# Spectral and gated mixer: the opening in a written order, S1 and S2 ahead of S3 and S4, and four down blocks moved into the last plain call

## The chip, the core and the metric

The kernel runs on one core of a Trainium2 chip. The metric is device time of one execution in microseconds: a median of 3 runs of the kernel, and beside it one profiled execution, whose span runs from its first to its last instruction. Five engines work side by side, each taking its own instructions in order: TensorE (PE in the profile, its weight loads PEld), VectorE (DVE), ScalarE (ACT), GpSimd (POOL) and SyncE (SP), which here only issues transfers.

## The reference

```python
def _A_ref(x, w_r, w_i):              # B, S, D = 1, 2048, 576
    X = rfft2(x, axes=(-2, -1)) * (w_r + 1j * w_i)
    return irfft2(X, s=(S, D), axes=(-2, -1))

def _B_ref(x, w_gate, w_up, w_down):  # F = 4608
    g = einsum("bsd,df->bsf", x, w_gate)
    u = einsum("bsd,df->bsf", x, w_up)
    return einsum("bsf,fd->bsd", sigmoid(g) * u, w_down)

xn = layernorm(x, axis=-1)            # eps = 1e-5
return x + _A_ref(xn, w_r, w_i) + _B_ref(xn, w_gate, w_up, w_down)
```

The spectral part is done as matrix products with Fourier matrices late in the kernel and is not touched by the change.

## The kernel before

Everything is kept to float32 accuracy out of products in a shorter format: each operand is split into a rounded high part and a low part. ScalarE writes the high part (a copy that rounds), VectorE the low part (operand less high part). A contraction over half of D, 288, takes seven matmuls (the list STEPS of `prod`, L648): two blocks of 128 with high by high, low by high and high by low, and one last step, (2, 2), on a **remainder** block, in which the 32 columns that are left stand three times, as high, high and low.

The 2048 rows of x form two pairs of chunks of 512 rows, four tiles of 128 rows each. A tile is read to `acc` (L358); VectorE takes its mean and variance (L369, L370); `scales` (L374 on) makes factor and bias, with a square root on ScalarE; `prep_hi` (L420) normalises on ScalarE into the buffer `xa`; `rem_hi` and `rem_lo` (L402, L407) make the remainder part `rma` or `rm`. `fill` (L449 to L455) then transposes two tiles on TensorE into a pair of PSUM banks (tag "pp", two such pairs, shared with the down blocks and the spectral part): four transposes of the main columns and two of the remainder. ScalarE copies the main block (L453) and the remainder (L454) into the operand store `X`, and VectorE writes the low part (L455), which frees the pair.

The 36 column blocks of F are the units. For units 0 and 1 of each pair of chunks `plain` (L671 to L677) is called once for each chunk: four products, two for the gate (bank A or B) and two for the other factor (bank E), then a sigmoid, a multiplication and the two parts of h (`hh`, `hl`). In the first pair of chunks the calls are (unit 0, chunk 1), (1, 1), (0, 2), (1, 2), here called the first to the last plain call. From unit 2 on `unit` (L699 to L739) works on both chunks at once with seven products in place of eight, on the blocks A11, A12, A22 of X and the sums S1 = A21 + A22, S2 = S1 - A11, S3 = A11 - A21, S4 = A12 - S2. `sums` (L432 to L435) makes these in place in `xa`. S3 takes the place of A21 in X, so it is filled after the plain calls.

Two units' h go through `down` (L755): for one tile of 128 rows 12 matmuls with w_down into a pair of banks, the **down block**; VectorE adds it to `acc` (L759). There are eight for the first two units, one for each tile; before, all start in unit 2. Weights come raw by transfer (L238), are split by `parts` (L250 on ScalarE, L252 and L254 on VectorE) into `w`, and are written to HBM for the second pair. `w_down` goes the same way (L304, L309, L311).

The program is recorded in one order and a scheduler may move instructions of an engine against each other. `placed` and `keep_in_program_order` mark instructions that must keep the recorded order. `beside(i)` and `turn` run the side jobs (weights, fills, sums, additions) between the products of a call. Ahead of the first products TensorE multiplies identity matrices (L904, L922), whose results are not used.

## Time and profile before

| | |
|---|---|
| median of 3 runs | 1418.17 us (1417.57 to 1419.64) |
| the profiled execution: its time | 1417.6 us |
| its span | 1415.8 us |
| granted TensorE clock, mean | 0.999 |
| DVE busy | 1123.7 us, 79% of the span |
| ACT busy | 640.3 us, 45% |
| first instruction of the first identity matmul | 3.46 us |
| fourth plain call's last product, followed by unit 2's first | 50.07 us |
| first down block | 61.37 us |

A line of the order of time gives start, time, engine, source line, operation, what it writes and from what, with shapes; "x4" joins equal neighbours, and the bracket is the engine's idle time before and who ended it. A line of a stage gives its bounds and length, then busy time (and instructions) of PE, PEld, DVE, ACT and POOL, the granted clock, the share of DMA engines and GB/s. A line of a group has the least, median and longest duration in ns.

### The profile page before, as it was taken

How to read it: one execution, taken by the hardware profiler on the slowest of the kernel's cores; microseconds unless marked ns; L12 is line 12 of the kernel's file. 1: busy time of each engine (PE TensorE's matmuls, PEld its weight loads, DVE VectorE, ACT ScalarE, POOL GpSimd, SP SyncE). 2: the span in 40 equal slices, each digit the busy share in tenths (PEclk: the TensorE clock that was granted, in tenths of full speed). 3: DMA queues.
4: the chain of work that ended last, by engine and by line, in shares of the span. 5: the costliest groups of instructions: out<-in, count | busy, mean ns of one | idle time of the engine just before them, and what ended most of it. 6: DMA issues, size and time to landing. Idle time of an engine off the chain costs nothing. (4 is left out here: it accounts for less than half of the span.)

```text
span 1415.8 us, 20731 instructions
## 1 busy us (share of the span) xinstructions
PE 1400.5 (99%) x7883; PEld 1228.9 (87%) x7883; DVE 1123.7 (79%) x1736; ACT 640.3 (45%) x1035; POOL 3.3 (0%) x5
## 2 busy tenths in 40 slices
PE   7999999999999999999999999999999999999998
PEld 5888888888888888888888888888888889888887
DVE  7988888888888888789466888877878878777885
ACT  6644444444444444444245444434555534443431
POOL 0000000000000000000000000000000000000000
PEclk9999999999999999999999999999999999999999
DMA  7588677777777776665777777778888787776643
GB/s 251 194 330 306 257 271 261 271 261 270 262 270 261 272 262 243 246 250 176 274 213 237 225 234 222 219 244 266 274 269 271 241 278 223 242 221 205 194 127 84
DMA packets 131043, 342.54 MB, mean 242 GB/s; under 512 B 12192, under 2 KB 51648, under 8 KB 126208
## 3 DMA queue, kind: packets, MB, share of 16 engines
q1 hardware_dynamic: 130016, 339.91, 71.7%
q8 instruction: 62, 1.02, 0.3%
q10 hardware_dynamic: 928, 1.31, 0.3%
q14 instruction: 37, 0.30, 0.1%
HBM read 205.04 MB, written 136.13 MB: 241 GB/s over the span
## 5 line engine op out<-in xcount | busy, mean ns | idle before, releaser
L648 PE MATMUL pB<-X,w 128*128 128x512 f32 x1484 | 381.0, 394 | 0.9 <-ACT pB L699 0.5
L648 PEld LDWEIGHTS pB<-X,w 128*128 128x128 f32 x1484 | 267.4, 188 | 51.7 <-ACT v L712 1.3
L648 PE MATMUL pE<-X,w 128*128 128x512 f32 x1064 | 272.3, 392 | 0.1
L648 PE MATMUL pA<-X,w 128*128 128x512 f32 x1008 | 259.3, 392 | 1.8 <-DVE X L455 1.2
L648 PEld LDWEIGHTS pE<-X,w 128*128 128x128 f32 x1064 | 193.1, 188 | 35.1 <-DVE y L713 0.7
L648 PEld LDWEIGHTS pA<-X,w 128*128 128x128 f32 x1008 | 182.7, 188 | 35.2 <-DVE X L455 1.9
L755 PE MATMUL po<-wd,hh 128*128 128x288 f32 x1216 | 210.8, 295 | 0.0
L846 PEld LDWEIGHTS ps<-wf,hs 128*128 128x128 f32 x1260 | 188.6, 188 | 18.5 <-ACT qs L854 0.9
L846 PE MATMUL ps<-wf,hs 128*128 128x288 f32 x1260 | 202.0, 295 | 0.4 <-ACT qs L854 0.4
L755 PEld LDWEIGHTS po<-wd,hh 128*128 128x128 f32 x1216 | 184.2, 188 | 11.7 <-ACT hh L738 0.4
L759 DVE TENSOR_TENSOR acc<-acc,po 128x576 f32<-128x576 f32 x168 | 125.7, 749 | 65.4 <-PE po L755 64.9
L250 ACT ACTIVATE w<-raw 128x768 fp32r<-128x768 f32 (+1 forms) x106 | 100.9, 953 | 92.6 <-PE pE L648 36.5
L755 PE MATMUL po<-wd,hl 128*128 128x288 f32 x608 | 128.7, 293 | 0.0
L856 DVE TENSOR_TENSOR qs<-qs,ps 128x576 f32<-128x576 f32 x112 | 84.0, 750 | 25.4 <-PE ps L846 24.4
L755 PEld LDWEIGHTS po<-wd,hl 128*128 128x128 f32 x608 | 98.7, 189 | 0.0
L713 DVE TENSOR_TENSOR y<-v,pE 128x512 f32<-128x512 f32 x68 | 46.6, 686 | 50.3 <-ACT v L712 49.5
L733 DVE TENSOR_TENSOR y<-y,g 128x1024 f32<-128x1024 f32 x67 | 81.9, 1222 | 3.4 <-DVE y L732 0.5
L782 ACT ACTIVATE hs<-y 128x512 fp32r<-128x512 f32 x105 | 64.8, 629 | 43.4 <-DVE y L820 14.8
L252 DVE TENSOR_TENSOR w<-raw,w 128x512 fp32r<-128x512 f32 (+1 forms) x106 | 81.8, 772 | 3.2 <-ACT w L250 2.9
L856 DVE TENSOR_TENSOR acc<-acc,ps 128x576 f32<-128x576 f32 x90 | 67.4, 750 | 19.5 <-PE ps L846 18.6
L716 ACT ACTIVATE g<-pB 128x512 f32<-128x512 f32 x68 | 40.7, 598 | 91.3 <-PE pB L648 91.3
L712 ACT ACTIVATE v<-pB 128x512 f32<-128x512 f32 x68 | 40.6, 597 | 70.5 <-PE pB L648 70.2
(170 smaller groups left out, 1611.0 us busy)
## 6 DMA issues: line engine op xcount, KB each, us to landing
w<-wsp SPq DMA_DIRECT2D x246, 320.0 KB, 3.6
wsp<-w SPq DMA_DIRECT2D x34, 2240.0 KB, 7.8
raw<-in_w SPq DMA_DIRECT2D x34, 768.0 KB, 9.6
wdsp<-wd SPq DMA_DIRECT2D x36, 576.0 KB, 4.6
wf<-tsp SPq DMA_DIRECT2D x60, 288.0 KB, 3.5
wf<-wdsp SPq DMA_DIRECT2D x45, 288.0 KB, 3.9
std<-in_wd SPq DMA_DIRECT2D x36, 288.0 KB, 5.5
ri<-in_ri SPq DMA_DIRECT2D x16, 580.0 KB, 5.1
```

The costliest lines, as they stand in the source:

```text
L250: placed(nc.scalar.activation(o[:, :, :3, :], src, AF.Copy))
L252: placed(nc.vector.tensor_tensor(o[:, :, 3:, :], src[:, :, :KT, :], f32(o[:, :, :KT, :]), op=OP.subtract))
L648: nc.tensor.matmul(bank, w[:, sw, :], X[:, x, sx, :], start=start and j == 0, stop=stop and j == len(STEPS) - 1, skip_group_check=skip)
L712: nc.scalar.activation(v[:, 1], bank["B"], AF.Copy)
L713: nc.vector.tensor_tensor(y[:, 1], v[:, 1], bank["E"], op=OP.add)
L716: nc.scalar.activation(g[:, 1], bank["B"], AF.Sigmoid)
L733: nc.vector.tensor_tensor(y, y, g, op=OP.mult)
L755: nc.tensor.matmul(pd[:, b, :HD], h[i], w[k][b], start=g == 0 and n == 0, stop=g == G - 1 and n == 2)
L759: nc.vector.tensor_tensor(a, a, pd[:, :, :HD], op=OP.add)
L782: nc.scalar.activation(hs[:, 0], src, AF.Copy)
L846: nc.tensor.matmul(pd[:, i, :HD], h[:, a, m], w[:, b], start=q == 0, stop=q == 2)
L856: nc.vector.tensor_tensor(o, o, pd[:, :, :HD], op=OP.add)
```

## The change

It touches the code up to unit 2. Six things are done:

1. **Order of the first transfers.** The first raw weights, half (2, 4), are read after two tiles of x instead of after four; the other half after four.
2. **A written opening.** `opening` replaces the first two plain calls and what stood before them. While `strict` is set, `strictly` keeps products, transposes, copies and most small operations in the written order on their engine. The main columns of A11 and A12 are transposed and copied first (`lift`); the remainders of all four tiles follow later in one bank for each operand (`lift_rem`), in the middle of the first plain call. Two pairs of half groups of identity matmuls become 15 and 10 full ones.
3. **Scales.** The square root takes eps as its bias, so VectorE's addition is no longer ahead of it, and the second chunk has two groups of two tiles instead of one group of four.
4. **`plain_late`**, used for the first and third plain call: each of the four products does six steps, the low part of X last, and the four remainder steps come at the end. The third call's gate has half a pair of banks, so the first two gates come later.
5. **S1 and S2 ahead of S3 and S4.** `sums` is divided into `sums_12` and `sums_34`, and the fills of S3 and S4 follow in four steps. Both w_down blocks are made in the third call.
6. **Down blocks.** `pend` holds the four tiles of the first chunk in the last plain call, one for each of its four products, and only the other four in unit 2.

```diff
+    def strictly(ins):
+        if strict[0]:
+            tc.keep_in_program_order(ins)
...
+    LOW_LAST = ((0, 0), (1, 1), (0, 3), (1, 4), (3, 0), (4, 1))
...
+    def plain_late(u, c, beside, mid):
+
+        G_, bank = new_plain(u, c)
+        beside(-1)
+        for i, (b, k) in enumerate(((0, 1), (0, 2), (1, 1), (1, 2))):
+            prod(bank[b], *of_plain(u, c, b, k), k == 1, False, steps=LOW_LAST)
+            end()
+            mid(i)
+            if i < 3:
+                beside(i)
+        for b in range(2):
+            for k in (1, 2):
+                prod(bank[b], *of_plain(u, c, b, k), False, k == 2, steps=STEPS[-1:])
+            if b == 0 and (u, c) != (0, 0):
+                gate(G_, bank)
+        beside(3)
+        return G_, bank
...
-            nc.scalar.activation(w0, ve, AF.Sqrt)
-            nc.vector.reciprocal(r0, w0)
+            strictly(nc.scalar.activation(w1, mv[:, ts, 1], AF.Sqrt, bias=nmr[:, NT - 1:]))
+            strictly(nc.vector.tensor_scalar(ve, mv[:, ts, 1], EPS, -0.5, op0=OP.add, op1=OP.mult))
+            strictly(nc.vector.reciprocal(r0, w1))
...
-    for i in range(TPP):
-        new_acc(0, i)
-        if i in (TPC - 1, TPC + 1):
-            load_raw(i // TPC)
+    for todo in ((new_acc, 0, 0), (new_acc, 0, 1), (load_raw, 0, 2), (new_acc, 0, 2), (new_acc, 0, 3), (load_raw, 0, 0),
+                 (new_acc, 0, 4), (new_acc, 0, 5), (load_raw, 1, 2), (load_raw, 1, 0), (new_acc, 0, 6), (new_acc, 0, 7)):
+        todo[0](*todo[1:])
...
+        identity(15)
+        scaled(0, 0)
+        early(0, 2)
+        level(0, 0)
+        scaled(0, 1)
+        p1 = pair("px_A11")
+        p2 = [ps.tile([P, CW], F32, tag="bE", name=f"px_A12_{i}", bufs=2) for i in range(2)]
+        his, lows = both(0, 0, (p1[:, 0], p2[0]))
+        for f in his:
+            f()
+        identity(10)
+        level(0, 1)
+        next(W[0, 2])
...
+        for m in range(TPC):
+            rem_hi(m, 0, "rm34", TPC)
+        next(W[0, 0])
+        for m in range(TPC):
+            rem_lo(m, 0)
...
+        first = plain_late(0, 0, lambda i: None, mid)
+        load_raw(2)
+        keep_p(0)
...
+            if p == 0 and n == 3:
+                pend = [(0, 0, m) for m in range(TPC)]
...
-                for _ in range((0, 0, 2, 2, 0)[i] if p and n < 2 else 0):
+                for _ in range(int(i >= 0) if p == 0 else (0, 0, 2, 2, 0)[i] if n < 2 else 0):
...
-        pend = [(p, 0, m) for m in range(TPP)]
+        pend = [(p, 0, m) for m in range(0 if p else TPC, TPP)]
```

Three places show how instructions move. In the rows `xa` is a tile's normalised buffer, `px` a bank that transposes write, `rs` the small tile of the scales, `pA`, `pB`, `pE` and `pg` the banks of products, `po` a down block; "x12" counts equal neighbours.

ScalarE from the first square root, before:

```order
L378 ACTIVATE rs_230<-rs_230 128x2
L420 ACTIVATE xa_0_218<-acc,nmr,rstd 128x576
L420 ACTIVATE xa_1_219<-acc,nmr,rstd 128x576
L402 ACTIVATE rma_0_0_240<-xa_0_218 128x2x64
L402 ACTIVATE rma_1_0_243<-xa_1_219 128x2x64
L378 ACTIVATE rs_255<-rs_255 128x2
L453 ACTIVATE X<-px_A_0_264 128x2x256
L454 ACTIVATE X<-px_A_0_264 96x256
L453 ACTIVATE X<-px_A_0_274 128x2x256
L454 ACTIVATE X<-px_A_0_274 96x256
L420 ACTIVATE xa_2_220<-acc,nmr,rstd 128x576
```

and now:

```order
L372 ACTIVATE rs_225<-mv,nmr 128x2
L257 ACTIVATE w_200<-raw_182 128x2x384
L414 ACTIVATE xa_196<-acc,nmr,rstd 128x576
L414 ACTIVATE xa_197<-acc,nmr,rstd 128x576
L372 ACTIVATE rs_244<-mv,nmr 128x2
L437 ACTIVATE X<-px_A_252 128x2x256
L437 ACTIVATE X<-px_A_0_253 128x2x256
L414 ACTIVATE xa_198<-acc,nmr,rstd 128x576
L414 ACTIVATE xa_199<-acc,nmr,rstd 128x576
L437 ACTIVATE X<-px_A_252 128x2x256
```

The remainder parts (`rma`) and remainder copies (96x256) have left this stretch, and a weight conversion stands ahead of the first normalisation.

TensorE from the second group of identity matmuls to the end of the first plain call, before:

```order
L922 MATMUL b_195<-idr 128x512 x4
L449 MATMUL px_A_1_300<-idf,xa_2_220 128x128 x2
L449 MATMUL px_A_1_310<-idf,xa_2_220 128x128 x2
L450 MATMUL px_A_1_300<-idr,rma_2_0_289 96x128
L449 MATMUL px_A_1_300<-idf,xa_3_221 128x128 x2
L450 MATMUL px_A_1_300<-idr,rma_3_0_293 96x128
L450 MATMUL px_A_1_310<-idr,rma_2_0_289 96x128
L449 MATMUL px_A_1_310<-idf,xa_3_221 128x128 x2
L450 MATMUL px_A_1_310<-idr,rma_3_0_293 96x128
L648 MATMUL pA_0_351<-X,w_296 128x512 x14
L648 MATMUL pE_0_352<-X,w_296 128x512 x14
L648 MATMUL pB_0_452<-X,w_360 128x512 x14
```

and now, where `px_r` holds remainders:

```order
L934 MATMUL b_195<-idr 128x512 x10
L434 MATMUL px_A_252<-idf,xa_198 128x128 x2
L434 MATMUL px_A_252<-idf,xa_199 128x128 x2
L434 MATMUL px_A_1_254<-idf,xa_198 128x128 x2
L434 MATMUL px_A_1_254<-idf,xa_199 128x128 x2
L648 MATMUL pA_0_309<-X,w_200 128x512 x12
L648 MATMUL pE_0_310<-X,w_200 128x512 x6
L443 MATMUL px_r_331<-idr,rm_0_294 96x128
L443 MATMUL px_r_331<-idr,rm_0_296 96x128
```

and, behind the other transposes of this kind,

```order
L443 MATMUL px_r_331<-idr,rm_0_300 96x128
L648 MATMUL pE_0_310<-X,w_200 128x512 x6
L648 MATMUL pA_0_309<-X,w_200 128x512 x2
L648 MATMUL pE_0_310<-X,w_200 128x512 x2
L648 MATMUL pB_0_356<-X,w_201 128x512 x14
```

The remainder transposes of all four tiles now stand behind 18 product matmuls of the first call, and the 14 matmuls of a bank are 12 or 6 and 6, with the two remainder steps at the end.

TensorE in the last plain call (`pB_1`, `pE_1`) from the third of the moved down blocks, now (before, the last call held the S1 and S2 transposes and no down block):

```order
L648 MATMUL pE_1_568<-X,w_201 128x512 x4
L788 MATMUL po_2_642<-wd_526,hh_454 128x288 x4
L788 MATMUL po_2_642<-wd_526,hl_455 128x288 x2
L788 MATMUL po_2_642<-wd_528,hh_473 128x288 x4
L788 MATMUL po_2_642<-wd_528,hl_474 128x288 x2
L434 MATMUL px_S_1_660<-idf,xa_198 128x128 x2
L434 MATMUL px_S_1_660<-idf,xa_199 128x128 x2
L443 MATMUL px_S_1_660<-idr,rma_3_598 96x128
L443 MATMUL px_S_1_660<-idr,rma_3_631 96x128
L648 MATMUL pE_1_568<-X,w_201 128x512 x7
L648 MATMUL pA_705<-X,w_590 128x512 x3
```

and VectorE at the same place, up to the part that the S1 transposes wait for:

```order
L438 TENSOR_TENSOR X<-px_S_0_555,X 128x2x256
L792 TENSOR_TENSOR acc<-acc,po_0_577 128x576
L259 TENSOR_TENSOR w_590<-raw_352,w_590 128x3x256
L261 TENSOR_TENSOR w_590<-raw_352,w_590 32x3x128
L402 TENSOR_TENSOR rma_3_598<-xa_198,rma_3_598 128x2x32
L281 TENSOR_TENSOR raw_352<-raw_352 128x2x384
L792 TENSOR_TENSOR acc<-acc,po_1_610 128x576
L283 TENSOR_TENSOR raw_352<-raw_352 128x384
L261 TENSOR_TENSOR w_590<-raw_352,w_590 32x2x128
L284 TENSOR_TENSOR raw_352<-raw_352 128x384
L259 TENSOR_TENSOR w_590<-raw_352,w_590 128x2x256
L402 TENSOR_TENSOR rma_3_631<-xa_199,rma_3_631 128x2x32
```

The S1 transposes of tiles 2 and 3 (`xa_198`, `xa_199`) need the remainder part `rma_3_631`, which on VectorE now has two additions of down blocks (`acc`) and most of unit 2's weights (`w_590`) ahead of it; before, no addition stood there.

More of the change, by code (lines that the diff above doesn't have):

```diff
@@ L282, in make_w, with keep_p @@
         yield
[L284 to L291 removed]
+    def keep_p(f):
+        nc.sync.dma_start(wsp[f][:, :4 * 5 * P], f32(WS[f][:, :4]).rearrange("p a k m -> p (a k m)"))
     def get_w(u):
@@ new lines, in lift_rem, with fill @@
+    def lift_rem(k, ms, rest, srcs=None):
+        for j, m in enumerate(ms):
+            src = srcs[j] if srcs else XR[m, XP[k]]
+            strictly(nc.tensor.transpose(rest[:KR, j * P:(j + 1) * P].bitcast(F32R), src, idr))
+        o = X[:KR, XA[k], KT, ms[0] * P:(ms[-1] + 1) * P]
+        return lambda: strictly(nc.scalar.activation(o, rest[:KR, :len(ms) * P], AF.Copy))
+    def fill(k, mm):
+        pt = pair(f"px_{k}_{mm}")
+        hi, lo = lift(k, mm, pt[:, 0])
+        rest = lift_rem(k, (2 * mm, 2 * mm + 1), pt[:, 1])
+        hi()
+        rest()
+        lo()
@@ L923, in spectral_glu_kernel, with identity @@
-    for m in (2, 3):
-        prep(0, m, 0)
-    next(mk)
-    next(mk)
-    for k in ("A11", "A12"):
-        fill(0, k, 1)
-    for _ in mk:
-        pass
-    stats([acc[TPC + m] for m in range(TPC)], TPC, R["pool"], table=True)
+    idle = [True]
+    def identity(n):
+        for _ in range(n):
+            strictly(nc.tensor.matmul(b0, idr, eye, start=idle[0], stop=True, skip_group_check=True))
+            idle[0] = False
+    for m in range(TPC):
+        new_xs(m)
+    W = {}
+    for f in range(G):
+        w = new_w(f)
+        for i in (2, 0):
+            W[f, i] = parts(w, RAW[f][:, i:i + 2], i, 2)
@@ L1102, in turn @@
     def turn(n):
+        was, strict[0] = strict[0], False
         for _ in range(n):
@@ L1109, in turn @@
         sides[:] = [g for g in sides if next(g, sides) is not sides]
+        strict[0] = was
     def finish(*gs):
```

295 lines of the change are left out of this document (160 added, 135 removed).

## Prediction

> **What bounds the kernel now.** I read the busy times first, then busy time by stage, then the order of time on TensorE, and last the order of time of the engines that TensorE waits for in the opening.
>
> ```profile
> PE 1400.5 (99%) x7883; PEld 1228.9 (87%) x7883; DVE 1123.7 (79%) x1736; ACT 640.3 (45%) x1035; POOL 3.3 (0%) x5
> 50.00:60.00 10.00, 9.56 (x56) 7.68 (x55) 9.87 (x17) 8.05 (x17) 0.00 (x0) 1.00 0.70 276
> 100.00:1390.00 1290.00, 1287.30 (x7271) 1134.49 (x7270) 1027.84 (x1540) 576.73 (x920) 0.00 (x0) 1.00 0.73 244
> ```
>
> TensorE (first figure after a stage's length) is busy for 1287.3 of the 1290 us behind the opening, so a microsecond saved or lost on it in the opening moves the end by a microsecond. The order of instructions differs only in the opening and the units 2 to 4. VectorE (third figure) has almost no room from 50 to 60 us: it is the engine that could take back what TensorE gains.
>
> Order of time on TensorE (start, time, instruction, and in brackets the idle time before and its releaser):
>
> ```profile
> 3.46 7.06 PE L904 MATMUL b<-idr 128*128 128x512 f32 x21 [3.46 <-DMA idr<-c_id]
> 10.36 0.60 PE L449 MATMUL px_A<-idf,xa 128*128 128x128 f32 x4
> 10.71 0.30 PE L450 MATMUL px_A<-idr,rma 128*96 128x128 f32 x1
> ...
> 11.48 1.14 PE L922 MATMUL b<-idr 128*128 128x512 f32 x4
> 16.23 0.49 PE L648 MATMUL pA<-X,w 128*128 128x512 f32 x1 [0.34 <-ACT X L453]
> 17.52 3.25 PE L648 MATMUL pA<-X,w 128*128 128x512 f32 x13 [0.80 <-DVE X L455]
> ...
> 39.66 0.38 PE L449 MATMUL px_S<-idf,xa 128*128 128x128 f32 x2
> ...
> 40.21 1.84 PE L648 MATMUL pE<-X,w 128*128 128x512 f32 x7
> ...
> 53.65 0.44 PE L449 MATMUL px_S<-idf,xa 128*128 128x128 f32 x2 [0.44 <-DVE X L455]
> 61.37 0.69 PE L755 MATMUL po<-wd,hh 128*128 128x288 f32 x4
> ...
> 62.95 1.77 PE L648 MATMUL pB<-X,w 128*128 128x512 f32 x7
> 64.56 0.69 PE L755 MATMUL po<-wd,hh 128*128 128x288 f32 x4
> ...
> 67.75 0.69 PE L755 MATMUL po<-wd,hh 128*128 128x288 f32 x4
> ```
>
> Prices from it, start to start: a matmul of a product 1.61/7 = 0.23 us (62.95 to 64.56); a down block, 12 matmuls, 1.58 (61.37 to 62.95); a fill's six transposes 0.55 (39.66 to 40.21), of which four of the main columns take 0.28 to 0.35 (10.36 to 10.71), so one of the remainder about 0.13.
>
> Unit 2's last product ends at 67.75. From the first product matmul (16.23) to there lie 51.52 us: 161 product matmuls (37.0), twelve fills (6.6) and two down blocks (3.2), 46.8 of work. **4.7 us are lost**: waits of 0.80 and 0.44 above and many smaller ones, mostly because a strict FIFO has a transpose or product ahead whose operand comes late.
>
> **The start of the first product.** Rows of ScalarE, VectorE and the transfers:
>
> ```profile
> 7.32 1.63 ACT L420 ACTIVATE xa<-acc,nmr,rstd 128x576 f32<-128x576 f32 x2 [1.07 <-DVE nmr L392]
> 14.75 0.84 ACT L250 ACTIVATE w<-raw 128x768 fp32r<-128x768 f32 x1
> 15.58 0.60 ACT L453 ACTIVATE X<-px_A 128x512 fp32r<-128x512 f32 x1
> 8.12 0.77 DVE L369 BATCH_NORM_STATS2 st<-acc 128x6 f32<-128x288 f32 x2
> 6.28 0.17 DVE L379 RECIPROCAL rs<-rs 128x2 f32<-128x2 f32 x1 [0.27 <-ACT rs L378]
> 7.07 0.16 DVE L392 SCALAR_TENSOR_TENSOR nmr<-mv,rstd 128x2 f32<-128x2 f32 x1
> 2.14 0.43 SPq L358 DMA_DIRECT2D acc<-in_x  x1
> acc<-in_x SPq DMA_DIRECT2D x1, 288.0 KB, 5.5
> 2.61 0.43 SPq L238 DMA_DIRECT2D raw<-in_w  x1
> raw<-in_w SPq DMA_DIRECT2D x1, 384.0 KB, 6.0
> ```
>
> Before, the fourth tile of x lands at 2.14 + 5.5 = 7.64 and the first half of the weights at 2.61 + 6.0 = 8.61. The change puts that half third. If the transfers land in order, the half lands between 4.8 and 7.6 (I take 6.4), and the fourth tile is the fifth transfer with the same bytes before it, so 8.61. Its statistics run 8.9 to 9.7 and 0.2 for the aggregate; the square root 0.27; reciprocal to bias 7.23 - 6.28 less the scaling that is now done meanwhile (0.12), 0.83: 11.0. Two normalisations take 1.63: 12.8. Main transposes and their latency 0.5, the first copy to X 0.6: **first product at 14.0**. What fell away from this path: two remainder copies on ScalarE, the remainder transposes and their copies, which now follow later, so nothing but main columns stands ahead of 16.23's counterpart. The weight conversion (0.84), now ahead of the first normalisation, ends at 7.25 where the normalisation was free to start at 7.1, and costs 0.2 there, hidden since the fourth tile is later. Bounds: if the fourth tile still lands at 7.64, the copies to X on ScalarE end at 10.6 and the start is 13.5; if the weight half lands only at 8.61, ScalarE's FIFO holds the normalisations to 9.5 and the start is 15.5. The 15 + 10 identity matmuls end at 8.4 and about 12.3 at the pace of 11.48's row (0.29 each); they cost nothing, covered by the normalisations, but would from 0.33 each on.
>
> **What is lost after it.** The eight remainder transposes that stood before the first product now follow it: +1.0. The low steps go last in each product, so the 0.80 of X's low half disappears. I followed the new order row by row at these prices; waits that remain:
>
> - ahead of the second chunk's transposes for tiles 2 and 3, whose normalisations wait for a second square-root group: 0.65;
> - bank E is released only after a sigmoid table load, a sigmoid and a multiplication: 0.15; the remainder parts of the second chunk: 0.1;
> - the S1 transposes of tiles 2 and 3, on VectorE's remainder part of S2: 0.4, below;
> - S3's and S4's transposes, on pair buffers that VectorE's low parts free: four waits, 0.7 together;
> - switching between products and transposes, as the 46.8 above leaves it out: 0.5.
>
> Sum 2.5 instead of 4.7. **The down blocks** are moved, not saved: four times 1.58 = 6.3 us of TensorE lie earlier. Their additions are what loads VectorE:
>
> ```profile
> 38.30 0.46 DVE L433 TENSOR_TENSOR xa<-xa 128x288 f32<-128x288 f32 x1
> 38.68 0.45 DVE L434 TENSOR_TENSOR xa<-xa 128x288 f32<-128x288 f32 x1
> 45.18 0.96 DVE L252 TENSOR_TENSOR w<-raw,w 128x768 fp32r<-128x768 f32 x1 [0.28 <-ACT w L250]
> 52.31 0.69 DVE L675 TENSOR_TENSOR y<-g,pE 128x512 f32<-128x512 f32 x1
> 63.42 0.75 DVE L759 TENSOR_TENSOR acc<-acc,po 128x576 f32<-128x576 f32 x1
> 64.08 0.75 DVE L311 TENSOR_TENSOR wd<-std,wd 128x576 fp32r<-128x576 f32 x1
> ```
>
> From the first S2 sum (about 34.1) VectorE has no gap up to that remainder part: nine sums at 0.37 (38.30 to 38.68), six remainder parts at 0.14, five of 512 columns at 0.6 (two y, one h, two low parts of X), two w_down parts and two additions at 0.66 (63.42 to 64.08), and unit 2's weights, which took 45.18 to 52.31 before, 5.6 without 1.5 of other work between, of which 1.2 stands later here: 3.3 + 0.8 + 3.0 + 2.6 + 4.4 = 14.1, with small handovers 14.6, so 48.7. TensorE by its own work (105 products, 16 remainder and 20 main transposes, two fills, three down blocks, the waits above) is there at 48.3: the wait of 0.4. Behind it on TensorE stand the last call's seven products and unit 2. So the earlier down blocks cost 0.4 now, while without those in front TensorE would stand there earlier by 4.7 and wait longer: they are also the cover. One more square-root group, 1.1 us of VectorE, is in the 24 us before. Further on VectorE follows: I get the hand-over of unit 3's h at 92.0 and TensorE's use of it at 93.1.
>
> **The sum.** End of unit 2's last product at the same content: 14.0 + 46.8 + 1.0 + 2.5 = 64.3 against 67.75: **3.4 us earlier**. The profiled execution took 1417.6 (span 1415.8), so 1414.2 for its like; the median is 1418.17, 0.6 above, and I predict **1414.8**.
>
> **Rivals.** 0.2% is 2.8 us, about what a measurement of this kernel tells from no change.
>
> *More is gained*: of the 2.5 lost, the waits for VectorE and the switching half vanish, or the start is 13.5: 5.0 earlier, 1413.2. For it: 53.65 shows but 0.44 of such waits in all of S3 and S4. Against: VectorE has 2.7 us of additions more by then.
>
> *VectorE gives half back*: its handovers in the strict order cost 2 more; 1416.8. For it: 9.87 of 10 at 50 to 60. Against: each of its rows repeats its duration within a few per cent.
>
> *Slower*: the remainder part of S2 (tile 3) becomes the end of the path. VectorE's order there holds, one behind the other, operations that wait for ScalarE, which itself waits for TensorE's gates and products; each such wait stops all behind it, and the moved down blocks wait for w_down's parts and the pair buffers in the same queue. From 48.7 on each microsecond of lateness goes to the end; at 52.5 the gain is used up. Seven late gives 1421.8. For it: no gap to absorb anything for 14.6 us. Against: the kernel before, as full, has TensorE idle for only 0.44 there.
>
> *The clock falls.* The identity matmuls' rows show a slow start:
>
> ```profile
> L904 PE MATMUL b<-idr x21: 390/502/795, 3.5 to 10.0; 128*128 128x512 f32 x13, 64*128 64x512 f32 x8
> 7.04 1.49 PE L904 MATMUL b<-idr 128*128 128x512 f32 x4
> ```
>
> The longest takes twice the shortest (795 and 390 ns). If the pause from 12.3 to 14.0, with transposes alone, brings that back for as long as it lasted at first (3.46 to 7.04), half of 3.6 is lost: 1.8, giving 1416.6. Against: before, the pause ran from 12.6 to 16.23 and the 13 matmuls at 17.52 kept 0.24. [...]
>
> **How the numbers follow.** Forecast 0.50, more gained 0.25, half given back 0.10, clock 0.04, slower 0.11. The bounds, start 13.5 to 15.5 and losses 1.0 to 4.5, give gains from 5.4 to -0.1, 1412.8 to 1418.3; I take 1412.2 to 1418.4, which leaves out most of the slower case and the far end of the better one. Faster by over 0.2%: the better case and 0.43 of the forecast's 0.50 (its spread reaches below 2.8), 0.68; slower 0.11; the rest 0.21.
>
> **What would show it.** The first product near 14.0 and its thirteen followers without the 0.80; about 0.65 ahead of the second chunk's transposes of tiles 2 and 3; TensorE's wait on a remainder part near 48; VectorE without gaps from 34 to 65; unit 2's last product, with six down blocks and six matmuls of unit 3 done, near 72.0 (67.75 + 6.3 + 1.4 - 3.4). It is wrong if the fifth transfer lands well after 8.6, if TensorE waits over 4 us in all for VectorE between 40 and 65, or if the time is lost again behind unit 4.

## The result and the profile after

| | kernel before | changed kernel |
|---|---|---|
| median of 22 runs | 1418.0 us (1417.4 to 1420.77) | 1416.07 us (1415.27 to 1417.04) |
| ratio of the two | | 0.9982 (95% interval 0.9976 to 0.9988) |
| the profiled execution: its time | 1417.6 us | 1416.97 us |
| its span | 1415.8 us | 1415.2 us |
| DVE busy | 1123.7 us | 1124.5 us |

The change is faster by 1.9 us from median to median, where 3.4 were forecast. From mean to mean it is 2.4 us, the 0.18% of the ratio, whose interval reaches from 0.12% to 0.24%. The order of time on TensorE after the change, at the rows that answer to those shown of before:

```profile
12.92 1.07 PE L434 MATMUL px_A<-idf,xa 128*128 128x128 f32 x8
14.23 3.02 PE L648 MATMUL pA<-X,w 128*128 128x512 f32 x12 [0.25 <-ACT X L437]
...
18.45 0.69 PE L443 MATMUL px_r<-idr,rm 128*96 128x128 f32 x8
18.99 1.60 PE L648 MATMUL pE<-X,w 128*128 128x512 f32 x6
...
28.31 0.44 PE L434 MATMUL px_A<-idf,xa 128*128 128x128 f32 x2 [0.24 <-ACT xa L414]
29.07 0.88 PE L434 MATMUL px_A<-idf,xa 128*128 128x128 f32 x6 [0.32 <-ACT xa L414]
29.70 0.95 PE L648 MATMUL pE<-X,w 128*128 128x512 f32 x3
30.63 3.33 PE L648 MATMUL pg<-X,w 128*128 128x512 f32 x12
...
50.43 0.24 PE L443 MATMUL px_S<-idr,rma 128*96 128x128 f32 x1 [0.51 <-ACT w L257]
...
71.60 1.77 PE L648 MATMUL pE<-X,w 128*128 128x512 f32 x7
73.21 0.69 PE L788 MATMUL po<-wd,hh 128*128 128x288 f32 x4
...
92.60 1.75 PE L648 MATMUL pB<-X,w 128*128 128x512 f32 x7
94.19 0.69 PE L788 MATMUL po<-wd,hh 128*128 128x288 f32 x4
...
96.36 1.90 PE L648 MATMUL pB<-X,w 128*128 128x512 f32 x7 [0.43 <-ACT v L745]
98.10 0.70 PE L788 MATMUL po<-wd,hh 128*128 128x288 f32 x4
```

The reader is to see four things. The first product starts at 14.23 instead of 16.23, and the 0.80 behind it is gone. The eight remainder transposes behind 18 products cost 18.99 - 18.45 = 0.54. Unit 2's last product ends at 73.21. Six down blocks and six matmuls of unit 3 lie before that, against two blocks before the change; on equal content before would stand at 67.75 + 6.3 + 1.4 = 75.45, so the changed kernel is 2.24 ahead there. Then unit 4 has a wait of 0.43 that before does not have.

Which part of the way costs what is seen by adding, from the start of one matmul to the start of the next, all time from the first product to the second down block behind unit 2 (before 16.23 to 99.87, after the change, in the second profile of it that is told of below, 14.23 to 98.08), sorted by the bank written (worked out from the trace; a wait counts with the matmul ahead of it):

| written | before: matmuls, us | change: matmuls, us |
|---|---|---|
| products (`pA`, `pB`, `pE`, `pg`) | 252, 61.96 | 252, 60.17 |
| transposes of A blocks (`px_A`, `px_r`) | 24, 2.67 | 32, 3.41 |
| transposes of sums (`px_S`) | 48, 4.63 | 48, 5.39 |
| down blocks (`po`) | 108, 14.38 | 108, 14.88 |
| sum | 432, 83.64 | 440, 83.85 |

Behind its first product the changed kernel gains nothing in all: it spends 1.8 less on products, where waits such as the 0.80 are gone, and 2.0 more on transposes and down blocks. Most of the 2.0 is again waits, which now begin behind a transpose or a down block (0.32, 0.52 and 0.41), and the eight transposes more (0.53). What it keeps up to there is the earlier start.

### The profile page after: what moved, and what is told of

Its sections match the earlier page's. It is cut to its first block, busy times and chain, and to the rows that moved or that the text cites. A ratio compares the mean times of both kernels' runs of the same rounds, so it can differ in the third digit from the quotient of the medians.

```text
span 1415.2 us, 20728 instructions
## 1 busy us (share of the span) xinstructions
PE 1400.5 (99%) x7883; PEld 1229.7 (87%) x7883; DVE 1124.5 (79%) x1739; ACT 640.6 (45%) x1032; POOL 3.3 (0%) x5
## 5 line engine op out<-in xcount | busy, mean ns | idle before, releaser
L648 PE MATMUL pA<-X,w 128*128 128x512 f32 x994 | 256.4, 392 | 0.2 <-ACT X L437 0.2
L816 DVE TENSOR_TENSOR hs<-y,hs 128x512 fp32r<-128x512 f32 x105 | 70.9, 686 | 1.9 <-ACT hs L815 1.1
```

Source lines behind the costliest of these rows:

```text
L648: strictly(nc.tensor.matmul(bank, w[:, sw, :], X[:, x, sx, :], start=start and j == 0, stop=stop and j == len(steps) - 1, skip_group_check ...
L816: return lambda: nc.vector.tensor_tensor(hs[:, 1], src, f32(hs[:, 0]), op=OP.subtract)
```

## Experiments

Expectations are quoted as they were written. "The opening" in them is the time from the first identity product to the second down block behind unit 2. It turned out a poor measure, because the identity lands anywhere from 3.35 to 4.12 us without moving the first product; the readings below go by the first product instead, and the expectations' own figure for the opening is given where it missed. The kernel before ran beside each group; its medians were 1417.86, 1418.1 and 1417.94.

**1. The old order of the first transfers.**

```diff
-    ... (new_acc, 0, 1), (load_raw, 0, 2), (new_acc, 0, 2), (new_acc, 0, 3), (load_raw, 0, 0),
+    ... (new_acc, 0, 1), (new_acc, 0, 2), (new_acc, 0, 3), (load_raw, 0, 2), (load_raw, 0, 0),
```

> The changed kernel with the first transfers in the old order: the first weight half goes behind four tiles of x instead of two. The opening is measured from the first identity matmul to the second down block of units 2 and 3 (before 99.87 - 3.46 = 96.41 us, changed 98.10 - 4.12 = 93.98). Theory A, the weight conversion stands ahead of the normalisations on ScalarE and waits for its transfer: the first product starts 1.0 to 1.6 us later after the first identity matmul than in the changed kernel (10.1 there), and the opening is 94.6 to 95.6. Rival B, transfers share the bandwidth and land together whatever their order: the first product moves by less than 0.3 and the opening stays at 93.7 to 94.3. On the late first landing (identity matmul at 4.12 us against 3.46 before): if the new order causes it, this kernel starts at 3.4 to 3.6; if it differs from one execution to the next, it may start anywhere between.

One run: 1417.81 us. Its ScalarE and TensorE:

```profile
8.70 0.85 ACT L257 ACTIVATE w<-raw 128x768 fp32r<-128x768 f32 x1 [2.51 <-DMA raw<-in_w]
15.44 2.79 PE L648 MATMUL pA<-X,w 128*128 128x512 f32 x11 [0.25 <-ACT X L437]
```

ScalarE's queue stands 2.51 us before the weights, and the normalisations behind them are late: first product 15.44, 1.2 later than in the change, at the prediction's upper bound of 15.5. The identity came at 3.49, but at 3.36 in another execution of the unaltered change too (run 8), so the late 4.12 was one execution's. By the identity, theory A's measure, the first product is 1.8 later and the opening 95.76, both a little past its ranges; rival B is out. Of the 2.0 gained at the start the transfers' order carries 1.2, as far as one execution tells: here the conversion that waits for the weights starts at 8.70, and with the change's opening the first product itself lies anywhere from 14.23 to 15.12.

**2. All eight down blocks in unit 2 again.** The rest of the change stays.

```diff
-            if p == 0 and n == 3:
-                pend = [(0, 0, m) for m in range(TPC)]
...
-        pend = [(p, 0, m) for m in range(0 if p else TPC, TPP)]
+        pend = [(p, 0, m) for m in range(TPP)]
```

> The changed kernel with all eight down blocks of the first two units back in unit 2 on; the rest as changed. Theory A, the moved blocks load VectorE in the last plain call for little and take cover from units 3 and 4: without the move TensorE waits longer at the S1 to S4 transposes (1 to 3 us more between 45 and 65 us) but the 0.43 wait in unit 4 is gone; the opening of 93.98 becomes 94.5 to 96. Rival B, the move only costs, by VectorE's additions ahead of the remainder part and by the cover lost in unit 4: the opening becomes 92.8 to 93.5. Ratio to the kernel before 0.998 to 0.9995 by A, 0.997 to 0.998 by B.

Measured: 1418.43 us, ratio 1.0 (0.999 to 1.0009). TensorE's order of time, and the clock in short stretches (the third figure from the end is the granted clock):

```profile
49.86 0.49 PE L648 MATMUL pE<-X,w 128*128 128x512 f32 x1
52.10 0.59 PE L648 MATMUL pB<-X,w 128*128 128x512 f32 x1 [1.74 <-ACT pB L732]
52.49 1.05 PE L648 MATMUL pA<-X,w 128*128 128x512 f32 x2
53.34 2.67 PE L648 MATMUL pE<-X,w 128*128 128x512 f32 x6
```

```profile
51.44 0.61 ACT L732 ACTIVATE pB<-pA 128x512 f32<-128x512 f32 x1
```

```profile
52.25:52.50 0.25, 0.25 (x2) 0.15 (x3) 0.25 (x1) 0.25 (x2) 0.00 (x0) 0.73 0.00 0
52.50:55.75 3.25, 3.25 (x9) 2.52 (x8) 3.21 (x6) 0.66 (x2) 0.00 (x0) 0.50 0.97 408
55.75:56.00 0.25, 0.25 (x3) 0.15 (x2) 0.25 (x1) 0.00 (x0) 0.00 (x0) 0.94 1.01 430
```

Without the blocks in front TensorE reaches unit 2 earlier and waits 1.74 there for ScalarE's copy of a bank. That copy starts at 51.44, behind a conversion of unit 2's weights and three copies to X, on a ScalarE without idle time from 48 on. Then the granted clock is halved, 0.50, for 3.4 us (from 52.37 to 55.78, by the shares in the two quarter microseconds), which by estimate, half of 3.4, costs 1.7 more. Theory A was right that the blocks are cover; the clock took the loss past its range (the opening by its measure is 97.34). But not every run lost clock: the three at 1.0 took 1417.47 to 1417.88, the five at 0.998 1418.4 to 1419.34, and even the three gain next to nothing on the 1417.86 of the kernel before. Unit 4's wait is gone, because all eight blocks stand in units 2 and 3.

**3. The old order of steps in the late plain calls.**

```diff
-    LOW_LAST = ((0, 0), (1, 1), (0, 3), (1, 4), (3, 0), (4, 1))
+    LOW_LAST = ((0, 0), (3, 0), (0, 3), (1, 1), (4, 1), (1, 4))
```

> The changed kernel with the six steps of the late plain calls in the old order, the low part of X second instead of fifth; nothing else. Theory A, the low part of X is 0.65 to 1.0 us behind the high part on VectorE, so TensorE waits again after the first matmul: idle 0.3 to 0.8 us there, as the 0.80 before, and again 0.2 to 0.8 in the third call; the opening grows by 0.3 to 1.2. Rival B, the main block alone is now copied early enough that the low part is there in time: less than 0.2 more.

One run: 1416.96 us. The waits stand where theory A has them, the first a little under its 0.3:

```profile
15.44 2.79 PE L648 MATMUL pA<-X,w 128*128 128x512 f32 x11 [0.22 <-DVE X L438]
...
32.82 2.79 PE L648 MATMUL pg<-X,w 128*128 128x512 f32 x11 [0.72 <-DVE X L438]
```

The first product came at 14.71 here, 0.48 later than in the change. From it to the second down block behind unit 2 it takes 99.18 - 14.71 = 84.47, 0.6 more than in the change. The waits and this lengthening are shown for one execution; their effect on the end is not, since one run cannot price it.

**4. The kernel before with the four moved blocks alone.**

```diff
+                if n == 2:
+                    sides += [make_d(0), make_d(1)]
...
+            if p == 0 and n == 3:
+                pend = [(0, 0, m) for m in range(TPC)]
...
-        pend = [(p, 0, m) for m in range(TPP)]
+        pend = [(p, 0, m) for m in range(0 if p else TPC, TPP)]
```

> The kernel before with the fourth item of the change alone: four down blocks in the last plain call, with both w_down blocks made in the third call. Theory A, VectorE is nearly full there and the blocks bring no work off TensorE: the opening changes by -0.5 to +1.0 (96.4 before), with TensorE waits of 0.3 to 1.5 on remainder parts and pair buffers between 45 and 65 us. Rival B, the blocks fill TensorE where VectorE is behind, and the move is the source of the gain: the opening is 1.5 to 2.5 shorter, as in the changed kernel.

Measured: 1417.76 us, ratio 1.0001 (0.9991 to 1.001). So neither the blocks alone nor the rest alone gains; together they do. Theory A's opening came out (96.79), but its waits of 0.3 to 1.5 did not: the one there is 0.15. Its profile also shows a fall of the clock. The opening by stages, first in this kernel, then in the kernel before:

```profile
16.00:17.75 1.75, 0.95 (x3) 0.60 (x4) 1.71 (x5) 1.68 (x4) 0.00 (x0) 1.00 0.00 0
17.75:18.00 0.25, 0.25 (x3) 0.18 (x2) 0.25 (x2) 0.00 (x0) 0.00 (x0) 0.60 0.00 0
18.00:21.00 3.00, 3.00 (x9) 2.32 (x8) 2.87 (x9) 0.00 (x0) 0.00 (x0) 0.50 0.47 194
21.00:21.25 0.25, 0.25 (x2) 0.19 (x1) 0.25 (x2) 0.00 (x0) 0.00 (x0) 0.58 0.80 328
```

```profile
16.00:17.75 1.75, 0.72 (x2) 0.42 (x3) 1.71 (x4) 1.75 (x5) 0.00 (x0) 1.00 0.00 0
18.00:21.00 3.00, 3.00 (x15) 2.47 (x14) 2.87 (x9) 0.00 (x0) 0.00 (x0) 1.00 0.40 167
```

Up to there both kernels have the same order and the same pauses, yet here TensorE does nine matmuls from 18 to 21 us and there fifteen. The clock was halved for 3.4 us in this execution and not in the profiled one of before. In this execution it cost only about 0.6 in the end: the transposes behind `pB`'s 14 matmuls start 28.32 - 15.98 = 12.34 after the first product, in the kernel before 27.95 - 16.23 = 11.72, since before's waits of 0.28 and 0.14 for those matmuls' weights fall away here. Each run carries its mean granted clock. All runs of the kernel before that were made beside experiments, but for one of 2300.2 us, and those of the change (first and second time):

| mean granted clock | before: runs, median us | change: runs, median us |
|---|---|---|
| 0.997 | 24, 1419.30 | 0 |
| 0.998 | 23, 1417.97 | 0 |
| 0.999 and 1.0 | 37, 1417.67 | 32, 1416.1 |

From the first row to the last lie 1.6 us. Of the fourteen profiled executions the twelve without a halved stretch before their last matmuls have means of 0.9990 to 0.9999, and the two with one 0.9981 and 0.9988; one stretch takes half of 3.4 us from 1416, 0.0012. So a run at 0.998 has lost about one stretch, and one at 0.997 more than one. That is an estimate from these means, for no profile of a run at 0.997 is kept. The next run tests whether the pauses of the opening are the cause.

**5. The kernel before with TensorE kept busy in its pauses.** Nine more identity products; their results are not used.

```diff
-    for n in range(4):
+    for n in range(8):
         tc.keep_in_program_order(nc.tensor.matmul(b0, idr, eye, start=False, stop=True, skip_group_check=True))
...
     for k in ("A11", "A12"):
         fill(0, k, 1)
+        tc.keep_in_program_order(nc.tensor.matmul(b0, idr, eye, start=False, stop=True, skip_group_check=True))
```

and four behind the first matmul of unit 0's first product.

> The kernel before, with nine more identity products put into TensorE's pauses ahead of its second product (four more between the two sets of transposes, one among the transposes of the second set, one behind them, and four behind the first product of unit 0), none of which anything waits for. Theory A (the kernel before loses a stretch of half clock in some executions, because TensorE does little from 12.6 to 17.5 us there, and this loss, which the change does not have, is a part of what the change gained): no run has a mean granted clock under 0.999, no run is above 1418.6 us, and the median is 1417.4 to 1417.6, 0.3 to 0.5 us under the kernel before. Theory B (the clock falls for a cause outside the opening, and the four slow runs in twenty of the kernel before have nothing to do with its pauses): about a quarter of the runs has a clock of 0.997 and a time above 1418.8, and the median is that of the kernel before.

Measured: 1417.46 us (1416.91 to 1418.22), ratio 0.9993 (0.9984 to 1.0002); none of 11 runs has a clock under 0.999, against 25 of the 33 of before beside it. Theory A; the median is 0.64 under the kernel before, more than its 0.3 to 0.5. The ratio's interval holds 1, but the long runs (15 of those 33 at 1418.97 and more) have no counterpart. So the pauses cost the kernel before some clock in a part of its executions. What the change gains by not losing it can be estimated from the table: from all 84 runs to the 37 at 0.999 and 1.0 it is 0.3 us by the medians (1417.96 to 1417.67) and 0.6 by the means.

**6. The second square root ahead of the copy.** In the change, ScalarE and VectorE around the second chunk's transposes:

```profile
25.59 0.60 ACT L437 ACTIVATE X<-px_A 128x512 fp32r<-128x512 f32 x1 [2.50 <-PE px_A L434]
26.08 0.29 ACT L372 ACTIVATE rs<-mv,nmr 128x2 f32<-128x2 f32 x1
```

```profile
26.40 0.17 DVE L374 RECIPROCAL rs<-rs 128x2 f32<-128x2 f32 x1 [1.23 <-ACT rs L372]
```

ScalarE stood idle for 2.50 us ahead of a copy with the ready square root behind it.

```diff
-        his[0]()
         scaled(1, 1)
+        his[0]()
         his[1]()
```

> The change, with the statistics and scales of the second chunk's tiles 2 and 3 issued ahead of the first X copy of that chunk, so that ScalarE's square root no longer stands behind a copy that waits for TensorE. Theory A (the two waits of the second chunk's second set of transposes, 0.24 and 0.32 us, come from that order and set the end): both waits are gone, the opening from the first identity product to the second down block behind unit 2 is 93.2 to 93.5 us in place of 94.0, and the time is 0.4 to 0.7 us under the change, 1415.4 to 1415.7. Theory B (the wait is only passed on: the next one, the remainder part of S2 at about 50 us, or unit 4's, grows by as much): opening 93.9 to 94.1, time 1416.0 to 1416.2.

Measured: 1415.43 us, ratio 0.9976 (0.9967 to 0.9984), against 1416.18 for the unaltered change beside it (run 8). The waits of 0.24 and 0.32 are gone, and from the first product to the second down block it takes 97.39 - 14.38 = 83.01 in place of 83.85. By time that is theory A; by the identity the opening is 94.02, 0.7 less than in run 8, though the number itself lies in theory B's range. The 0.65 that the prediction had placed there was real and set the end. Two waits with brackets of 0.56 together were worth 0.84 from start to start: a wait costs more than its bracket says, which the account of the prediction below comes back to.

**7. Two of the four blocks left in unit 2.**

```diff
-                pend = [(0, 0, m) for m in range(TPC)]
+                pend = [(0, 0, m) for m in range(2)]
...
-        pend = [(p, 0, m) for m in range(0 if p else TPC, TPP)]
+        pend = [(p, 0, m) for m in range(0 if p else 2, TPP)]
```

> The change, with two of the four down blocks left in unit 2 and two in the last plain call. Theory A (each block covers work of VectorE and ScalarE where it stands, so its place is a trade between the wait at 50 us, which was 0.51 with four blocks there and 1.74 with none, and unit 4's wait, which was 0.43 with four blocks left for units 2 and 3 and none with eight): unit 4's wait is 0 to 0.25, the wait near 50 us is 0.7 to 1.3, and the time is 1416.2 to 1417.3. Theory B (what counts is only that some block stands there): both waits as in the change or smaller, time 1415.7 to 1416.1.

Measured: 1415.75 us, ratio 0.998 (0.9971 to 0.9989). Unit 4's product follows its down block without a wait:

```profile
96.60 0.42 PE L788 MATMUL po<-wd,hl 128*128 128x288 f32 x2
96.86 1.77 PE L648 MATMUL pB<-X,w 128*128 128x512 f32 x7
```

and the wait near 50 is 0.41, not larger. These are theory B's numbers. Theory A was right about unit 4 and wrong about the trade: two blocks cover the third call's end as well as four. Unit 4's wait belongs to the blocks that no longer stand in units 2 and 3. In the change ScalarE's queue has a weight conversion ahead of `v`, which waits for VectorE:

```profile
94.98 0.85 ACT L257 ACTIVATE w<-raw 128x768 fp32r<-128x768 f32 x1 [1.58 <-DVE raw L281]
95.73 0.58 ACT L745 ACTIVATE v<-pB 128x512 f32<-128x512 f32 x1
```

**8. The change once more.**

> The change once more, unaltered, for a second profile and for times on this chip. Theory A (the first product's 14.23 us held one execution's late first landing, 4.12 us against 3.46, and the order of TensorE's work fixes the rest): the first identity product starts at 3.3 to 3.6, the first product of unit 0 10.1 to 10.4 us after it or later by what the fourth tile or the first weights land late, the opening from the first identity product to the second down block behind unit 2 is 93.8 to 94.3, all clocks are 0.999 or 1.0, and the time is 1415.8 to 1416.4. Theory B (the new order of the first loads lands the identity late each time): first identity product at 4.0 to 4.2 again.

Measured: 1416.18 us, ratio 0.9983 (0.9974 to 0.9992); the identity at 3.36, and the first product again at 14.23. Theory A, but for the opening as measured from the identity, 94.72: the identity does not set the start.

**9. The bridged kernel before with the moved blocks.** The edits of run 5 and run 4 together.

> The kernel before with the nine identity products of e5_bridged in TensorE's pauses, so that the clock stays up, and with the four moved down blocks (both w_down blocks made in the third plain call). Beside e5_bridged (1417.46) it gives the price of the moved blocks alone without the half-clock stretch that lay in the profile of e4_downs_alone. Theory A (the moved blocks gain little by themselves, since what they cover here is only 0.4 to 0.6 us of waits ahead of S3's and S4's transposes; their worth is as cover for the shortened opening): 1416.9 to 1417.5. Theory B (without the clock's fall the blocks alone gain what the change gains behind its first product, a microsecond or more): 1416.0 to 1416.6.

Measured: 1417.42 us, ratio 0.9995 (0.9986 to 1.0004), beside 1417.46 of run 5. With the clock up in all runs the moved blocks alone are worth nothing that can be measured. Theory A.

**10. Three waits taken away at once.** Runs 6, 7 and 11 together.

> The change with three edits: the second square root of the second chunk ahead of the X copy (e6_sqrt_first), two of the four down blocks left in unit 2 (e7_two_early), and the S1 and S2 sums of two tiles in one side step, so that VectorE makes the remainder part of tile 3 ahead of the first weights of unit 2 that now precede it. Theory A (the three waits are independent: 0.75 of the one, 0.4 of unit 4's, 0.4 of the remainder part): no wait over 0.2 us between 25 and 100 us and 1414.4 to 1414.9. Theory B (with the opening shorter the same queues are late elsewhere, and the gains overlap): 1415.0 to 1415.5 with a wait of 0.3 to 0.8 at another place from 45 to 100 us.

Measured: 1414.73 us (1414.47 to 1415.77), ratio 0.9978 (0.9969 to 0.9986). TensorE has no wait over 0.2 us behind its first product up to 100 us, and from there to the second down block behind unit 2 it takes 82.45. That is theory A, and the best version of this study: 1.45 under the change's 1416.18 of run 8, which was measured on another chip, where the kernel before took 1418.1 against 1417.94 here.

**11. The sums of two tiles in one step.** TensorE's order stays; VectorE makes the remainder part of tile 3 earlier.

```diff
             for m in (2 * mm, 2 * mm + 1):
                 sums_12(m)
-                yield
+            yield
+            yield
```

> The change with the S1 and S2 sums of two tiles in one side step instead of two, which alters nothing in TensorE's order and moves VectorE's remainder part of tile 3 ahead of an addition and three conversions of unit 2's weights. Theory A (TensorE's wait of 0.51 us at 50.43 is for that part, whatever the bracket names, and sets the end): the wait is gone, and the time is 0.3 to 0.5 us under the change, 1415.6 to 1415.9. Theory B (the wait is for ScalarE's weight copy, as the bracket says, or unit 2's weights are then late in turn): a wait of 0.3 or more stays between 49 and 53 us, and the time is 1416.0 to 1416.3.

Measured: 1416.42 us, ratio 0.9987 (0.9978 to 0.9996).

```profile
50.09 0.37 PE L443 MATMUL px_S<-idr,rma 128*96 128x128 f32 x2
...
53.17 0.80 PE L788 MATMUL po<-wd,hh 128*128 128x288 f32 x4 [0.38 <-DVE acc L792]
```

The wait at 50 is gone, so it was for VectorE's part and not for the ScalarE copy in the bracket. But the fourth down block now waits 0.38 for its pair of banks, which VectorE's addition frees, and the first product to the fifth down block takes 67.22 - 14.65 = 52.57 against 52.60. The result is theory B's, no gain, but by neither of its reasons: alone, the cure passes the wait on to the pair of banks. In run 10, where only two blocks stand there, it does not.

**12. The change without its written order.**

```diff
-    strict = [True]
+    strict = [False]
```

> The change without its written order: the marks that keep the recorded order in the opening are dropped, all else is as in the change. ScalarE then makes four remainder parts (about 0.2 us each beyond their latency) ahead of the X copies that the first product waits for, and TensorE's identity matmuls stand 17, 2 and 6 instead of 15 and 10. Theory A (the written order is a part of the gain because it keeps the first chunk's remainder parts off ScalarE until the main columns are copied): first product 0.4 to 0.9 us later than in the change, and 1416.5 to 1417.2. Theory B (the recorded order alone carries the gain, and the marks do nothing that can be measured): first product within 0.2 of 14.23 and 1415.9 to 1416.4.

Measured: 1415.48 us (1414.99 to 1419.01), ratio 0.9985 (0.9976 to 0.9994). Both theories are wrong. The start is later than A had it, and the time is lower than B had it:

```profile
13.45 1.42 PE L434 MATMUL px_A<-idf,xa 128*128 128x128 f32 x8 [1.68 <-ACT xa L414]
15.82 3.03 PE L648 MATMUL pA<-X,w 128*128 128x512 f32 x12 [0.96 <-ACT X L437]
...
52.09 0.80 PE L788 MATMUL po<-wd,hh 128*128 128x288 f32 x4 [0.36 <-DVE acc L792]
```

```profile
11.06 0.69 DVE L438 TENSOR_TENSOR X<-px_A,X 128x512 fp32r<-128x512 f32 x1
11.67 0.15 DVE L386 SCALAR_TENSOR_TENSOR rstd<-rs 128x2 f32<-128x2 f32 x1
11.74 0.68 DVE L438 TENSOR_TENSOR X<-px_A,X 128x512 fp32r<-128x512 f32 x1
12.34 0.15 DVE L387 SCALAR_TENSOR_TENSOR nmr<-mv,rstd 128x2 f32<-128x2 f32 x1
```

The first product comes 1.6 later: VectorE puts two low parts of X into the chain of scales, 1.0, and its statistics of the third tile start 0.5 later (8.22 against 7.71 in run 8). ScalarE's remainder parts cost 0.1. But from there to the second down block behind unit 2 it takes 97.57 - 15.82 = 81.75, which is 2.1 less than in the change: the scheduler has both square roots of the second chunk side by side ahead of the copies, and unit 4's wait is gone. By the waits of run 8, counted with their edges as below (0.93 and 0.68), these two are most of it. Two of its ten runs have clocks under 0.999, 1419.01 and 1416.77. The long pause ahead of the first product, 1.68 and 0.96, is back and may be why; no profile of these two runs shows it. Keeping the written order up to the first product only was not tried.

## Why the prediction came out as it did

It said 1414.8 and faster; 1416.07 and faster was measured, in the range. It had put 0.68 on a gain of over 0.2%, 2.8 us; what came, 1.9 to 2.4, lies in the case that it gave 0.21. By its steps:

- **The start**: 14.0 predicted, 14.23 in both profiles of the change. From the fourth tile's statistics on it came by the chain that was named: the bias is ready at 11.02 (predicted 11.0) and the tiles are normalised at 12.69 (predicted 12.8, though its 11.0 and 1.63 add up to 12.6). Ahead of that the chain was another. In the change's first profile the fourth tile landed at 8.03, not at 8.61, and nothing waited for it: its statistics start at 8.70 (in run 8 at 8.69) behind those of the third tile, which start at 7.73 and 7.71. In five profiles with this opening, the change's two and those of runs 7, 10 and 11, the first product comes 6.50 to 6.52 us after the third tile's statistics start, and these start anywhere from 7.71 to 8.60. So a miss of only 0.23 is in part luck. With the old order of transfers it was 15.44 against the upper bound of 15.5, by the way that the prediction gave for that bound: ScalarE's normalisations start at 9.45, and 9.5 had been said.
- **The remainder transposes**: +1.0 predicted, 0.54 measured. In a row of eight each costs 0.07, about half of the 0.13 that was taken from transposes mixed with others.
- **The step that was furthest off** is the 2.0 of waits left behind the first product. The prediction priced matmuls from start to start and took waits from the brackets, and a bracket prints less than a wait costs. Before, the one matmul at 16.23 has its successor at 17.52: 1.29 in place of 0.23, so 1.06 is lost where the bracket says 0.80. In the profiles the idle time begins at the modelled end of the last matmul, 0.39 after its start, which is 0.16 later than its successor starts in a row. And the first product matmul behind a wait takes 0.34 to its successor's start, 0.11 more. So a wait costs some 0.27 beyond its bracket, and one under 0.16 has no bracket at all.
- **Before's 4.7**, counted in this way, are 4.3 of waits, whose brackets hold only 2.37, and 0.5 at the nine places where products follow transposes, whose first matmul takes 0.28 to 0.32. So "waits ... and many smaller ones" was right, and so was the size of the 0.5 for switching, for which the prediction showed no row. (The two sum to 0.1 more than 4.7 because its prices are rounded up.)
- **The changed kernel's loss** by the same prices is 73.21 - 14.23 - 6.3 - 1.4 - 46.8 = 4.5 beyond the work, where 2.5 and the 1.0 of the remainder transposes had been forecast. In its second profile 2.7 of it are waits (brackets: 1.2), 0.9 the first matmuls behind transposes, at now twelve places, 0.5 the remainder transposes, and 0.4 is not assigned. By the list: the second chunk's transposes 0.93 for 0.65, the S1 transposes 0.67 for 0.4, the second chunk's remainder parts 0.13 for 0.1, S3 and S4 0.29 for 0.7, bank E nothing for 0.15. Not on the list are 0.56 in the third call, whose first product waits for ScalarE's copy and VectorE's low part of X; from 29.70 to 30.63 three matmuls take 0.93 in place of 0.68, of which 0.16 is such a wait, and no bracket shows it. The last 0.11 is the very first product's. The terms together, start, waits, switching, remainder and the rest: 0.23 + 0.7 + 0.4 - 0.5 + 0.4 = 1.2, and 3.4 - 1.2 is the 2.2 measured at unit 2.
- **Unit 4**: the prediction followed h up to unit 4 and found no wait. The wait of 0.43 is on another thing, `v`, behind a weight conversion in ScalarE's queue. Run 7 shows that it is the price of taking four down blocks out of units 2 and 3: with two taken out it is gone. "They are also the cover" was said of the place that the blocks went to (run 2 bears it out) and not of the place that they left.
- **From the profile to the median**: 0.6 was added because before's median of three runs stood that far above its profiled execution. The 37 runs of before at 0.999 and 1.0 have a median only 0.1 above it, so most of the 0.6 is likely the clock, and the change has no run under 0.999. With the 1.2 above and 0.4 for unit 4, 1414.2 + 1.2 + 0.4 = 1415.8 stands against 1416.07 and, the second time, 1416.18, with 1416.03 for that second profiled execution. Of the first profiled execution's smaller difference, 0.6, a part came late: its last matmuls start 0.8 after those of the second profile, though the two stand together at the start and at 98 us.
- **The clock rival** had the wrong sign. It asked whether the changed kernel's pause would halve the clock and took the 0.24 of the 13 matmuls behind before's pause as evidence that this one did not. One execution could not tell: 47 of 84 runs of before are under 0.999, and the 24 at 0.997 take 1.6 us more than those at 0.999 and 1.0. That the changed kernel's shorter pause keeps the clock was the author's estimate; the 32 runs of the change, none under 0.999, agree with it.
- **The slower rival** did not come: the remainder part held TensorE up by 0.7 from start to start (bracket 0.5), not by 4, and run 11 shows that even this was no bound of its own. *Half given back*, 1416.8, is the rival that came nearest, but of its 2 us of late handovers only 0.7 of waits beyond the forecast came, and a part of them is ScalarE's.

What stays open is why the first product behind transposes or behind a wait takes longer, where the last 0.4 goes, and whether a written order that ends at the first product would join run 12's 81.75 to the change's 14.23. The new scales, S1 and S2 ahead of S3 and S4, and the later remainders were not tried alone, so what each of them gives is not shown.

## What to carry to other kernels

Price waits as matmuls are priced, from start to start: the idle time that a profile prints is only a part of what a wait costs on TensorE here (0.80 printed and 1.06 lost at before's first product), and by the estimate above waits under 0.16 print none. A piece of work that is moved takes cover away from where it stood and gives it where it goes, so both places must be read, and both halves of the change tried alone: here each half alone gained nothing, one of them in part because of the clock, and the two together 2 us. Read the granted clock of many executions and not of the profiled one only: here more than half of those of the kernel before, 47 of 84, are under 0.999, and the profiled one is not.

## What the hardware showed

- In the two profiles in which the granted clock falls before the last matmuls it is halved, 0.50, for 3.4 us: 52.37 to 55.78 in run 2 and 17.80 to 21.21 in run 4, from the quarter-microsecond stretches. In run 2 the 3.4 us ahead of the fall hold 1.7 us of product matmuls and one wait of 1.74.
- The length of a pause does not decide alone. In before's profiled execution the 3.61 us from 12.62 to 16.23 hold transposes and no product or identity matmul, and up to 17.52 only one more matmul of 0.49 follows. That is longer, and holds fewer product matmuls, than the 3.4 us of run 2, and yet the clock stayed at 1.00 up to 24 us; run 4, with the same order and the same pauses, lost it at 17.80. 47 of 84 runs of before have a mean clock under 0.999, and with identity matmuls in these pauses (run 5) none of 11. What else decides, no run here tells.
- A 128x512 product matmul has its successor 0.23 us after its start in a row, 0.34 when it is the first behind a wait (0.335 to 0.343, five times in before's profile up to unit 2) and 0.28 to 0.32 when it is the first behind transposes.
- Transfers of the first microseconds land at different times from one execution to the next: the identity lets TensorE start from 3.35 (run 7) to 4.12 (the change), with the change's opening the third tile's statistics start from 7.71 (run 8) to 8.60 (run 7), both behind a wait for its transfer, and the first product comes from 14.23 (run 8) to 15.12 (run 7). A single run cannot price less than a microsecond in an opening.
